# A windowed-attention and SwiGLU kernel: three warm-up matmuls rather than four, a fetch cut into head pairs, and other steps for weight casts, wo's powers and output stores

## The chip, the cores and the metric

The kernel runs on one core of a Trainium2 chip. The metric is the device time of one execution in microseconds (us); the profile that is read here shows one such execution, taken by the hardware profiler. The engines are TensorE (PE in the profile: matmuls; PEld: its weight loads), VectorE (DVE), ScalarE (ACT), GpSimd (POOL) and SyncE (SP), which here issues nearly all DMAs.

## The reference

x is 2048 tokens by 512 features, in fp32. Both branches read the same layer-normalised x.

```python
xn = _layernorm(x, axis=-1)
s = _A_ref(xn, A_wqkv, A_wo)        # 32 heads of 16
g = _silu(_B_ref(xn, B_w1, B_w3, B_w2))
return x + s * g
# _A_ref: q, k, v = xn @ wqkv;  scores = q k^T * 16 ** -0.5,
#   kept where 0 <= idx_q - idx_k < 256;  softmax over keys;  (p v) @ wo
# _B_ref: (silu(xn @ w1) * (xn @ w3)) @ w2,  1792 columns between
```

## The kernel before

**Precision.** A product of fp32 matrices is made of three fp16 matmuls: high by high, low by high and high by low halves (XH and XL are the halves of the normalised, transposed x). A weight tensor or a block of it is first scaled by a power of two. This power is measured on the chip: sums of squares per partition (`squares`, on ACT at line 249 and on DVE at line 251) go through a bf16 cast (line 261, DVE) and a small matmul with ones (`powers`, lines 280 and 285, PE), and a chain of small DVE instructions (lines 291 to 304) makes the power. Then the tensor is cut into halves. `split` does it in two instructions (line 333 on ACT, 334 on DVE); `split_pool` scales in place and casts the high half on ACT (lines 342 and 343) and makes the low half in four pieces on POOL (line 345).

**Tiling.** The tokens stand in 4 tiles of 512 (t). Attention has 4 groups of 8 heads (g), each with 2 passes of head pairs (p): 32 units (t, g, p). Q and K of a group are projected (`project`, matmuls at line 597, emptied at 614 by ACT and 618 by DVE), stored to DRAM in an expanded form (lines 619 to 625) and fetched back as tiles qa and KA (`fetch`, line 641). The first pass over the scores (`pass1`, matmuls at 665) finds row maxima on DVE (line 679); the second makes scores again (746), exponentials on ACT (756) and the product with V (774). The feed-forward branch works on 14 blocks of 128 columns (f): gate and up matmuls at 1036, emptied through ACT 1051, DVE 1055 and 1060 and ACT 1069; the down product is at 1261 for the first two token tiles and, with folded weights, at 1179 for the others. wo's product is at 1313.

**What sets the order.** PE's order is written by hand: a list of dense matmul pieces is spread between the score batches, and each piece is a step. `later(n, f)` runs f's code n steps on; `beside_scores(n, f)` puts f's small matmuls beside the first score batch after n steps. The other engines are ordered by a scheduler: it places an instruction by when it becomes ready, and by its place in the program where several are. `tc.issue_after(ins)` gives the instructions under it an order edge behind `ins`. The name `lasts["emptied"]` is set where a matmul bank is emptied, always to a DVE instruction (at line 618, for example).

**Buffers.** Two matmul banks (m) alternate, two double score tiles (s) alternate, and there is one more (po). 54 slots in SBUF hold weights and intermediate tiles: `take` gives the slot that has been free for longest, `give` frees one, some steps later where it says `after`. SP issues DMAs in order.

**The places that the change touches.** The prologue (from line 1531) runs warm-up matmuls with no useful product (`keep_busy`, line 1537), turns x by transposes (line 493, copied to XH by ACT at 496 and to XL by DVE at 501) and projects K and Q of group 0: k00 takes a score tile (line 594), q00 an m bank. `measure(f)` measures a pair of weight blocks f and f + 1 and calls `cut` four times, two for each block, at the steps that a tuple gives. `wout` prepares wo in unit 7. `total` (from line 1300) makes the output and stores it. The loads of w1 and w3 are at line 868, those of the later wqkv columns at 395, the stores of cut weights at 1042.

Of the kernel before, what the change touches and what calls it, by code (L numbers as in the profile page):

```python
# [10 lines left out]
F32 = mybir.dt.float32  # L11
# [10 lines left out]
P = 128  # L22
# [4 lines left out]
DH = 16  # L27
# [56 lines left out]
def tile_block(ctx: ExitStack, tc: tile.TileContext, x, wqkv, wo, w1, w3, w2, out):  # L84
# [35 lines left out]
    def give(*tiles, after=0):  # L120

        for made in tiles:
            given[0] += 1
            free.append((now[0] + after, given[0], held.pop(id(made))[0]))
# [38 lines left out]
    def bank(shape, dtype=F32):  # L163

        open_bank[0] = b = 1 - open_bank[0]
        return psm.tile(shape, dtype, name=f"m{b}", tag=f"m{b}", bufs=1)
# [414 lines left out]
    def project(t, g, k, terms=(range(3),), scores_bank=False):  # L581


        cell = {}

        parts = ([[(c, i) for c in (2 * half, 2 * half + 1) for i in range(3)] for half in range(2)] if len(terms) == 1
                 else [[(c, i) for i in group for c in range(NC)] for group in terms])

        def part(n):
            assert turned[t] == 4  # L590
            w = WQ[t, g, k]
            xh, xl = X[t]
            if n == 0:
                cell["pp"] = pss.tile([P, 2, TW], F32, name="s")[:, 0, :] if scores_bank else bank([P, TW])
            for c, i in parts[n]:
                a, b = ((0, xh), (1, xh), (0, xl))[i]
                nc.tensor.matmul(cell["pp"], w[:, (a * NC + c) * P:(a * NC + c + 1) * P], b[:, c, :], start=(c, i) == parts[0][0],  # L597
                                 stop=(c, i) == parts[-1][-1])
            if n < len(parts) - 1:
                return  # L600
            if t == 0:
                def store():
                    with behind_load():
                        nc.sync.dma_start(dWQ[g, k], w)
                    give(w, after=8)
                later(45, store)
            else:
                give(w)
            pp = cell["pp"]
            both = take(F16)  # L610
            B = both.rearrange("p (a t) -> p a t", a=2)
            s = QS / (XS * WS)
            with urgent():
                nc.scalar.activation(B[:, 0, :], pp, AF.Copy, scale=s)

            def rest():
                with urgent():
                    lasts["emptied"] = nc.vector.scalar_tensor_tensor(B[:, 1, :], pp, s, B[:, 0, :], op0=ALU.mult, op1=ALU.subtract)  # L618
                d = (dQ, dK)[k][g][:, :, t * TW:(t + 1) * TW]
                if k == 0:  # L620
                    nc.sync.dma_start(d[:, 0:2, :], B[:, 0:1, :].to_broadcast([P, 2, TW]))
                    nc.sync.dma_start(d[:, 2, :], B[:, 1, :])
                else:
                    nc.sync.dma_start(d[:, 0:2, :], B)
                    nc.sync.dma_start(d[:, 2, :], B[:, 0, :])
                give(both, after=4)
            later(1, rest)
        return opening([(len(l), lambda n=n: part(n)) for n, l in enumerate(parts)])
# [2 lines left out]
        WQ[t, g, k] = w = take(F16)  # L631
        nc.sync.dma_start(w, dWQ[g, k])

    def fetch(t, g):
        QA[t, g] = qa = qpool.tile([P, 4, TW], F16, name="qa")
        ka = keys(t, g)
        c0 = 0 if t else 2 * P
        for dst, d in ((ka[:, :, c0:], dK[g][:, :, t * TW - 2 * P + c0:(t + 1) * TW]),
                       (qa, dQ[g][:, :, t * TW:(t + 1) * TW])):
            for r in range(2):  # L640
                lasts["load"] = nc.sync.dma_start(dst[64 * r:64 * r + KR],
                                  d[64 * r:64 * r + 64].rearrange("(a d) i t -> (d i) a t", d=DH))

# [224 lines left out]

    measured = set()

    def measure(f, apart=0):

        raws = [RAW.pop(f + i) for i in range(2)]
        sb = squares([raws[0][0], raws[1][0], raws[0][1], raws[1][1]], on_act=4 if f > 2 else 2, apart=apart)

        def scale(s=None):
            pp = small.tile([P, 2, 2], F32, name="pp")
            pi = small.tile([P, 2, 2], F32, name="pi")  # L880
            return then(s, powers(sb, 4, pp.rearrange("p a b -> p (a b)"), pi.rearrange("p a b -> p (a b)"), s),
                        lambda: rest(pp, pi))

        def rest(pp, pi):
            ff = slice(f, f + 2)
            nc.vector.tensor_scalar(sg_scale[:, ff], pp[:, 0, :], 0.5 / (WS * XS), None, op0=ALU.mult)
            nc.vector.tensor_mul(p13[:, ff], pp[:, 0, :], pp[:, 1, :])
            measured.update((f, f + 1))

            def cut(i, k):  # L890
                if k == 0:
                    WF[0, f + i] = [[None, None], WF.pop((0, f + i), [None, None])[1]]
                WF[0, f + i][0][k] = a = take(F16)
                split_pool(a[:, 0:D], a[:, D:], raws[i][k], pi[:, k, i:i + 1])
                give(raws[i][k], after=5)
            for i in range(2):
                for k in range(2):
                    later(((1, 2, 4, 6) if f < 8 else (1, 5, 9, 13))[2 * i + k], lambda i=i, k=k: cut(i, k))
        if started:
            beside_scores(8, scale)  # L900
        else:
            later(10 if apart else 6, scale)

# [389 lines left out]
    def total(t, b):  # L1293

        r = slice(t * TW + b * P, t * TW + (b + 1) * P)
        cell = {}

        def part(half):
            WOH, WOL = SQ["wo"][:2]
            tb = slice(b * P, (b + 1) * P)  # L1300
            if half == 0:
                cell["ps"] = bank([P, D])
                assert (t, b) in summed
                cell["y"] = y = take(F32)
                acc = ACC[t, b]
                with behind_exp():
                    nc.scalar.activation(y, acc, AF.Tanh, scale=0.5)
                nc.vector.scalar_tensor_tensor(y, y, 1.0, acc, op0=ALU.add, op1=ALU.mult)
                give(acc)
            ps, y = cell["ps"], cell["y"]  # L1310
            for g in (2 * half, 2 * half + 1):
                for i, (a, w) in enumerate(((0, WOH), (0, WOL), (1, WOH))):
                    nc.tensor.matmul(ps, O[t, g][:, a, tb], w[g], start=g == 0 and i == 0,  # L1313
                                     stop=g == NG - 1 and i == 2)
            if half:
                with urgent():
                    lasts["emptied"] = nc.vector.scalar_tensor_tensor(y, ps, sc["y"], y, op0=ALU.mult, op1=ALU.mult)
                if t == NT - 1:
                    nc.vector.tensor_add(y, y, XR[t, b])
                else:  # L1320
                    halves(nc.gpsimd.tensor_add, y, y, XR[t, b])

                def store():
                    nc.sync.dma_start(out[r, :], y)
                    give(y, XR[t, b], after=30)
                if t == NT - 1:
                    store()
                else:
                    later(4, store)
                if b == 3:  # L1330
                    give(*(OT[t, g] for g in range(NG)))
        return opening([(6, lambda h=h: part(h)) for h in range(2)])
# [22 lines left out]
    def feed_forward():  # L1355
# [4 lines left out]
        for t in range(NT):  # L1360
            for f in range(FB):
                if t == 0:
# [3 lines left out]
                    elif f + LEAD == FB - 1:  # L1366
                        pieces += [(0, lambda f=f: load(0, f)) for f in range(FB - 2, FB)]
                    if f % 2 and f + 3 < FB:
                        pieces.append((0, lambda f=f + 3: later(5, lambda: measure(f, 1)) if f == 6 else measure(f, 1)))
                    pieces += [(0, lambda f=f: load_down(0, f)) for f in range(f + 2 if f else 0, min(f + 3, FB))]  # L1370
                    for m in range(f + 1 if f else 0, min(f + 2, FB)):
                        k = next(k for k, (_, f1) in enumerate(GROUPS) if m < f1)
# [158 lines left out]
        nc.gpsimd.memset(KA[2][:, a, :].bitcast(F32), TWO_ONES)  # L1531


    def keep_busy(n):
        ps = bank([P, 4, P])
        for _ in range(n):
            nc.tensor.matmul(ps, onesb, onesb.unsqueeze(1).to_broadcast([P, 4, P]), start=True, stop=True)

# [19 lines left out]
        flush()  # L1558
    with tc.issue_after(lasts["hi"].ins), tc.issue_after(lasts["x"].ins):
        qk[1][1]()  # L1560
    keep_busy(4)


    k00, q00 = (project(0, 0, k, ((0,), (1,), (2,)), k) for k in (1, 0))
    run([k00[0], q00[0], k00[1]])
    qk[1][2]()
    with tc.issue_after(lasts["scale"].ins):
# [2 lines left out]
    qk[1][3]()  # L1570
    with tc.issue_after(lasts["hi"].ins):
        run([k00[2], q00[2]])
    later(1, lambda: fetch(0, 0))
    k01 = project(0, 1, 1, ((0, 2), (1,)))
    run(k01[:1])
    wv[2]()
# [4 lines left out]
    sc["o"] = scaled(SQ["wv"][3], OS / WS, "so")  # L1581
    with tc.issue_after(lasts["hi"].ins):
        measure(0)
    run(project(0, 1, 0, scores_bank=True))
    later(1, lambda: fetch(0, 1))
    run(value(0, True))
    qk[2][1]()
# [35 lines left out]
    for n, u in enumerate(units):  # L1623
# [7 lines left out]
            wout[0]()  # L1631
        if n == 7:
            wout[1](2)
            beside_scores(12, lambda s: then(s, wout[2](s), lambda: later(2, lambda: wout[3](2)), lambda: later(3, out_scale)))
        want += a_unit - other[n]
        mine = more(want)

# [39 lines left out]
```

## Time and profile before

| | us |
|---|---|
| median of three runs | 811.76 |
| the three runs | 811.22, 811.76, 811.85 |
| the profiled execution | 811.24 |
| its span (first to last instruction) | 809.4 |
| PE busy in the span | 793.7 |
| DVE, ACT, POOL busy | 631.2, 392.1, 377.1 |
| granted TensorE clock | 1.00 |

1.84 us of the profiled execution lie outside the span. A timeline row shows start, duration, engine, line and operation, output and inputs, and in brackets the idle time of the engine just before it with what ended it. Matmul rows that follow one another are joined with a count (x4); their durations overlap, since a matmul starts before the one ahead of it has left the array. SPq stands for SP's queue of DMA issues.

### The profile page before, as it was taken

Reading aid. Unit: us, or ns where it says so; the run is one execution under the profiler, and the core shown is the slowest. Engines: PE = TensorE matmul, PEld = TensorE weight load, DVE = VectorE, ACT = ScalarE, POOL = GpSimd, SP = SyncE. Lnnn points to the kernel's source line nnn. Section 1 sums busy time; section 2 is a strip of 40 time slices with the busy share of each in tenths; the row PEclk is TensorE's granted clock in tenths of the full one; section 3 lists DMA queues with packets and bytes.
Section 4 is the critical chain, followed back from the end, with each engine's and each line's share of the span. In section 5 each row is a group of like instructions: output and inputs, shape, how many; then the busy total and the mean of one; then the engine's idle time right before and its main releaser. Section 6 shows DMA issues by size and latency. Waiting matters only on the chain.

```text
span 809.4 us, 23944 instructions
## 1 busy us (share of the span) xinstructions
PE 793.7 (98%) x9176; PEld 403.7 (50%) x9176; DVE 631.2 (78%) x2037; ACT 392.1 (48%) x591; POOL 377.1 (47%) x732
## 2 busy tenths in 40 slices
PE   8999989999999999999999999999999999999998
PEld 4444444444444444444444454456544754466465
DVE  8788788887888777887988888777778787875437
ACT  6879586553546544345344433344444234344411
POOL 2345376342329445354353455530346276550670
PEclk9999999999999999999999999999999999999999
DMA  9968554835576474757655634646372644335321
GB/s 282 265 214 267 160 183 134 278 114 191 160 199 208 134 232 139 218 142 263 160 162 181 194 104 119 185 137 179 105 201 74 160 139 137 113 90 172 111 65 62
DMA packets 109795, 134.19 MB, mean 166 GB/s; under 512 B 18864, under 2 KB 64880, under 8 KB 109680
## 3 DMA queue, kind: packets, MB, share of 16 engines
q1 hardware_dynamic: 109392, 132.13, 54.6%
q8 instruction: 72, 1.18, 0.6%
q10 hardware_dynamic: 288, 0.52, 0.2%
q14 instruction: 43, 0.35, 0.1%
HBM read 91.23 MB, written 36.57 MB: 158 GB/s over the span
## 4 chain that ended last, share of the span: by engine, by line
PE 79%; DVE 8%; ACT 6%; DMA 3%; issue 2%; SPq 1%; POOL 0%; ACTq 0%; DVEq 0%
PE m L1036 30%; PE po L774 8%; PE m L1261 8%; PE m L1179 8%; PE m L597 7%; PE s L746 5%; PE m L1313 4%; PE m L567 4%; PE s L665 3%; DMA slot<-in_B_w_dram 2%; DVE junk L679 2%; PE po L665 2%; ACT slot L342 1%; ACT pt L756 1%; ACT sqa L249 1%
## 5 line engine op out<-in xcount | busy, mean ns | idle before, releaser
L1036 PE MATMUL m<-XH,slot 128*128 128x512 f16 x896 | 267.4, 380 | 1.6 <-DVE slot L618 1.2
L756 ACT ACTIVATE pt<-s,es 128x1024 f32<-128x1024 f32 x152 | 167.5, 1112 | 193.7 <-DVE s L753 186.5
L1036 PEld LDWEIGHTS <-slot 128*128 128x128 f16 x1344 | 124.7, 98 | 156.0 <-issue 12.0
L1036 PE MATMUL m<-XL,slot 128*128 128x512 f16 x448 | 169.9, 379 | 0.0
L753 DVE TENSOR_TENSOR s<-s,MK 128x256 f32<-128x256 f32 (+2 forms) x280 | 118.7, 434 | 51.2 <-PE s L746 47.0
L679 DVE CUSTOM_DVE_ANT_0 junk<-s,MW 128x320 bf16<-128x320 f32 x276 | 133.9, 485 | 17.9 <-PE s L665 10.3
L339 POOL TENSOR_TENSOR slot<-slot,slot 128x256 f16<-128x256 f32 (+1 forms) x86 | 57.7, 692 | 141.9 <-ACT slot L1069 76.7
L345 POOL TENSOR_TENSOR slot<-slot,slot 128x128 f16<-128x128 f32 x168 | 69.1, 446 | 58.3 <-ACT slot L343 58.3
L679 DVE CUSTOM_DVE_ANT_0 junk<-po,MW 128x320 bf16<-128x320 f32 x172 | 83.4, 485 | 4.7 <-DVE mt L704 0.3
L1261 PE MATMUL m<-slot,slot 128*128 128x512 f16 x336 | 78.6, 380 | 0.3 <-DVE slot L1055 0.3
L774 PE MATMUL po<-pt,V 64*32 64x320 f32 (+4 forms) x2880 | 77.2, 342 | 0.8 <-DVE pp L304 0.8
L597 PE MATMUL m<-XH,slot 128*128 128x512 f16 x240 | 71.0, 380 | 1.6 <-DVE slot L1055 1.2
L1179 PE MATMUL m<-slot,slot 128*128 128x256 f16 x588 | 68.4, 273 | 0.0
L1094 POOL TENSOR_TENSOR slot<-slot,slot 128x256 f16<-128x256 f32 x98 | 64.6, 671 | 1.1
L1051 ACT ACTIVATE slot<-m,sgs 128x512 f32<-128x512 f32 x56 | 38.3, 683 | 54.4 <-PE m L1036 52.3
L774 PEld LDWEIGHTS po<-pt,V 64*32 64x32 f32 x2880 | 50.5, 106 | 22.9 <-PE s L515 0.9
L1179 PEld LDWEIGHTS <-slot 128*128 128x128 f16 x588 | 56.1, 98 | 11.5 <-issue 3.0
L1055 DVE SCALAR_TENSOR_TENSOR slot<-slot,m 128x512 f32<-128x512 f32 x56 | 38.3, 684 | 29.0 <-ACT slot L1051 29.0
L746 PE MATMUL s<-qa,KA 50*64 50x320 f16 (+3 forms) x1472 | 58.4, 260 | 0.1
L597 PEld LDWEIGHTS <-slot 128*128 128x128 f16 x384 | 35.6, 98 | 44.8 <-issue 3.4
L746 PEld LDWEIGHTS <-KA 50*64 50x64 f16 x1472 | 30.1, 106 | 51.9 <-issue 30.9
L1261 PEld LDWEIGHTS <-slot 128*128 128x128 f16 x336 | 30.7, 98 | 38.6 <-issue 4.2
(189 smaller groups left out, 1138.5 us busy)
## 6 DMA issues: line engine op xcount, KB each, us to landing
slot<-dW SPq DMA_DIRECT2D x98, 256.0 KB
slot<-in_B_w_dram SPq DMA_DIRECT2D x56, 256.0 KB
slot<-dFold SPq DMA_DIRECT2D x48, 256.0 KB
dW<-slot SPq DMA_DIRECT2D x42, 256.0 KB
slot<-in_A_x_dram SPq DMA_DIRECT2D x30, 256.0 KB
KA<-dK SPq DMA_DIRECT2D x24, 288.0 KB
qa<-dQ SPq DMA_DIRECT2D x32, 192.0 KB
slot<-dWQ SPq DMA_DIRECT2D x24, 256.0 KB
```

What stands on the lines that cost most here:

```text
L339: op(out[:, c], a[:, c], b[:, c])
L345: nc.gpsimd.tensor_sub(lo[:, c:c + P], raw[:, c:c + P], hi[:, c:c + P])
L597: nc.tensor.matmul(cell["pp"], w[:, (a * NC + c) * P:(a * NC + c + 1) * P], b[:, c, :], start=(c, i) == parts[0][0], stop=(c, i) == parts[ ...
L679: lasts["maximum"] = nc.vector.tensor_tensor_reduce(out=junk[:, :n], in0=s[:, r, :n], in1=mask, scale=1.0, scalar=NEG, op0=ALU.add, op1=AL ...
L746: nc.tensor.matmul(s[64 * h:64 * h + 64, r, o:o + 64 * n], ka[rows, 2 * p + a, 64 * (m + 4):64 * (m + 5)], qa[rows, 2 * p + a, 64 * (m + k ...
L753: nc.vector.tensor_add(v, v, MK[:, kind, of:of + n, :].unsqueeze(1).to_broadcast([P, 2 * len(which), n, 64]))
L756: lasts["exp"] = nc.scalar.activation(pt, s, AF.Exp, scale=es)
L774: nc.tensor.matmul(cell["po"][32 * i:32 * i + 32, h, 64 * (m + k):64 * (m + k + n)], V[64 * h:64 * h + 64, (4 * t + m // 2) % VB, hd * VW: ...
L1036: nc.tensor.matmul(cell[k], w[:, (a * NC + c) * P:(a * NC + c + 1) * P], b[:, c, :], start=c == 0 and i == 0, stop=c == NC - 1 and i == 2)
L1094: nc.gpsimd.tensor_sub(lo, view, hi)
L1179: nc.tensor.matmul(cell["ps"][:, c], made[:, f:f + P], wj[:, g:g + 256], start=j == j0 and c == 0 and n == 0, stop=j == j1 - 1 and n == 2, ...
L1261: nc.tensor.matmul(ps, hh[:, a * TW + b * P:a * TW + (b + 1) * P], w[:, c * D:(c + 1) * D], start=f == f0 and i == 0, stop=f == f1 - 1 and ...
```

## The change

The diff, cut to what the rest of the text speaks of; the projections `k00`, `q00` and the one at line 1584 pass their bank in another way, with the same bank as before.

```diff
-    def fetch(t, g):
+    def fetch(t, g, ps=None):
...
-        for dst, d in ((ka[:, :, c0:], dK[g][:, :, t * TW - 2 * P + c0:(t + 1) * TW]),
-                       (qa, dQ[g][:, :, t * TW:(t + 1) * TW])):
-            for r in range(2):
-                lasts["load"] = nc.sync.dma_start(dst[64 * r:64 * r + KR],
-                                  d[64 * r:64 * r + 64].rearrange("(a d) i t -> (d i) a t", d=DH))
+        for heads in (slice(0, 4),) if ps is None else [slice(2 * p, 2 * p + 2) for p in ps]:
+            for dst, d in ((ka[:, heads, c0:], dK[g][:, :, t * TW - 2 * P + c0:(t + 1) * TW]),
+                           (qa[:, heads, :], dQ[g][:, :, t * TW:(t + 1) * TW])):
+                for r in range(2):
+                    rows = slice(64 * r + DH * heads.start, 64 * r + DH * heads.stop)
+                    lasts["load"] = nc.sync.dma_start(dst[64 * r:64 * r + KR],
+                                      d[rows].rearrange("(a d) i t -> (d i) a t", d=DH))
...
-    def measure(f, apart=0):
+    def measure(f, apart=0, until=8):
...
+            def tied(i, k):
+                with tc.issue_after(lasts["emptied"].ins):
+                    cut(i, k)
             for i in range(2):
                 for k in range(2):
-                    later(((1, 2, 4, 6) if f < 8 else (1, 5, 9, 13))[2 * i + k], lambda i=i, k=k: cut(i, k))
+                    if f < 8:
+                        later((1, 2, 4, 6)[2 * i + k], lambda i=i, k=k: cut(i, k))
+                    else:
+                        later((1, 4, 13, 16)[2 * i + k], lambda i=i, k=k: tied(i, k))
         if started:
-            beside_scores(8, scale)
+            beside_scores(until, scale)
...
-                    later(4, store)
+                    later(10, store)
...
-                        pieces.append((0, lambda f=f + 3: later(5, lambda: measure(f, 1)) if f == 6 else measure(f, 1)))
+                        pieces.append((0, lambda f=f + 3: later(8, lambda: measure(f, 1, 6)) if f == 6 else measure(f, 1)))
...
-    keep_busy(4)
+    waiting = scores_bank()
+    keep_busy(3, waiting[:, 0, :].rearrange("p (k q) -> p k q", q=P))
...
-    later(1, lambda: fetch(0, 0))
+    later(1, lambda: fetch(0, 0, (0, 1)))
...
-            beside_scores(12, lambda s: then(s, wout[2](s), lambda: later(2, lambda: wout[3](2)), lambda: later(3, out_scale)))
+            beside_scores(14, lambda s: then(s, wout[2](s), lambda: later(2, lambda: wout[3](2)), lambda: later(3, out_scale)))
```

So the change does six things. Three warm-up matmuls, written to the score tile that k00 takes next, stand where four stood in an m bank. The first fetch, of group 0, loads KA and qa for two head pairs apart: 8 loads of half the size rather than 4. The measuring of the pair of blocks 6 and 7 begins 8 steps on rather than 5, and its small matmuls stand beside the first batch after 6 further steps rather than 8. The cuts of blocks 8 to 13 move from steps 1, 5, 9 and 13 to 1, 4, 13 and 16, under an order edge behind the last emptying of a bank. wo's powers move from 12 steps on to 14. Output stores of the first three token tiles are issued 10 steps on rather than 4.

Lines after the first hunks are up to 9 higher in the changed kernel (641 is 643, 679 is 681, 868 is 870, 1055 is 1063). The places at which its instructions stand otherwise follow.

SP's queue at the first fetch (dK and dQ are Q and K of a group in DRAM; 143, 147: group 0; 144, 148: group 1). Before:

```order
L625 DMA dK_147<-slot_408 128x512
L621 DMA dQ_143<-slot_417 128x2x512
L624 DMA dK_147<-slot_408 128x2x512
L622 DMA dQ_143<-slot_417 128x512
L395 DMA slot_551<-in_A_wqkv_dram 128x4x128
L625 DMA dK_148<-slot_462 128x512
L641 DMA KA_140<-dK_147 48x4x512 x2
L641 DMA qa<-dQ_143 48x4x512 x2
L624 DMA dK_148<-slot_462 128x2x512
```

And in the changed kernel, where the two load rows are followed by two more that read the same, for the second head pair:

```order
L625 DMA dK_147<-slot_406 128x512
L624 DMA dK_147<-slot_406 128x2x512
L621 DMA dQ_143<-slot_415 128x2x512
L622 DMA dQ_143<-slot_415 128x512
L625 DMA dK_148<-slot_464 128x512
L643 DMA KA_140<-dK_147 48x2x512 x2
L643 DMA qa<-dQ_143 48x2x512 x2
```

The load of a block of wqkv (395) no longer stands between the stores and the fetch; it is issued behind the stores of group 1, and so behind the fetch of both pairs.

DVE, around the bf16 cast of the squares of the second pair of blocks (sb, 128x2), in the first score batches. Before:

```order
L679 ISA junk,M<-s,M_106 128x256
L679 ISA M 128x1
L294 TENSOR_SCALAR al<-s 128x1
L261 CAST sb<-ssq 128x2
L679 ISA junk,M<-s,MW 128x320
L295 SCALAR_TENSOR_TENSOR al<-s,al 128x1
```

And in the changed kernel, some 18 rows further on:

```order
L334 SCALAR_TENSOR_TENSOR slot_726<-slot_205,sw_643,slot_726 128x512
L1063 SCALAR_TENSOR_TENSOR slot_737<-slot_737,m_716 128x512
L681 ISA junk,M<-s,MW 128x320
L681 ISA M 128x1
L261 CAST sb<-ssq 128x2
L681 ISA junk,M<-s,MW 128x320
```

The cast of sb is no longer ahead of four row maxima, two splits (334) and an emptying of a bank (1055, now 1063).

ACT, at the casts of a pair of blocks from 8 to 13 (a row in brackets names what the instruction waits for: an engine, or a landing of a DMA). Before:

```order
L1051 ACTIVATE slot_1827<-m_1805,sgs 128x512 [waits PE_49]
L342 ACTIVATE slot_1096<-slot_1096,pi 128x512 [waits DVE_49]
L342 ACTIVATE slot_1097<-slot_1097,pi 128x512
L343 CAST slot_1829<-slot_1096 128x512 [waits DMAHW7_49,Activation_49]
L343 CAST slot_1961<-slot_1097 128x512 [waits Activation_49,Pool_49]
L249 ACTIVATE sqa,ssq<-slot_1567 128x512 [waits DMAHW0_49]
L342 ACTIVATE slot_1100<-slot_1100,pi 128x512
L342 ACTIVATE slot_1101<-slot_1101,pi 128x512
L343 CAST slot_2064<-slot_1100 128x512 [waits Activation_49]
```

And in the changed kernel:

```order
L1059 ACTIVATE slot_1829<-m_1807,sgs 128x512 [waits PE_49]
L342 ACTIVATE slot_1098<-slot_1098,pi 128x512 [waits DVE_49]
L342 ACTIVATE slot_1099<-slot_1099,pi 128x512
L343 CAST slot_1831<-slot_1098 128x512 [waits DMAHW3_49,Activation_49]
L343 CAST slot_1916<-slot_1099 128x512 [waits DMAHW1_49,Activation_49]
L249 ACTIVATE sqa,ssq<-slot_1569 128x512 [waits DMAHW4_49]
L342 ACTIVATE slot_1102<-slot_1102,pi 128x512
L342 ACTIVATE slot_1103<-slot_1103,pi 128x512
L343 CAST slot_2171<-slot_1102 128x512 [waits DMAHW5_49,Activation_49]
```

The casts stand where they stood; they go to other slots, and two of them now wait for a landing of a DMA where they waited for POOL or for nothing outside ACT.

More of the change, by code (lines that the diff above doesn't have):

```diff
@@ L593, in part @@
             if n == 0:
-                cell["pp"] = pss.tile([P, 2, TW], F32, name="s")[:, 0, :] if scores_bank else bank([P, TW])
+                cell["pp"] = bank([P, TW]) if scores_bank is False else scores_bank()[:, 0, :]
             for c, i in parts[n]:
@@ L1531, in tile_block, with keep_busy @@
         nc.gpsimd.memset(KA[2][:, a, :].bitcast(F32), TWO_ONES)
-    def keep_busy(n):
-        ps = bank([P, 4, P])
+    def keep_busy(n, ps=None):
+        ps = bank([P, 4, P]) if ps is None else ps
         for _ in range(n):
@@ L1560, in tile_block @@
         qk[1][1]()
-    keep_busy(4)
-    k00, q00 = (project(0, 0, k, ((0,), (1,), (2,)), k) for k in (1, 0))
+    waiting = scores_bank()
+    keep_busy(3, waiting[:, 0, :].rearrange("p (k q) -> p k q", q=P))
+    k00, q00 = (project(0, 0, k, ((0,), (1,), (2,)), (lambda: waiting) if k else False) for k in (1, 0))
     run([k00[0], q00[0], k00[1]])
@@ L1583, in tile_block @@
         measure(0)
-    run(project(0, 1, 0, scores_bank=True))
+    run(project(0, 1, 0, scores_bank=scores_bank))
     later(1, lambda: fetch(0, 1))
```

## The prediction

> **What bounds the kernel now.** The page comes first: PE is busy for 98% of the span.
>
> ```profile
> span 809.4 us, 23944 instructions
> PE 793.7 (98%) x9176; PEld 403.7 (50%) x9176; DVE 631.2 (78%) x2037; ACT 392.1 (48%) x591; POOL 377.1 (47%) x732
> ```
>
> So 15.7 us of the span (809.4 - 793.7) are without a matmul, and nothing but these can be won, as the change removes one matmul of 0.22 us. The table of stretches shows where they lie.
>
> ```profile
> 40.00:60.00 20.00, 18.90 (x134) 8.05 (x133) 16.83 (x72) 15.60 (x35) 9.84 (x20) 1.00 0.69 217
> 60.00:80.00 20.00, 18.70 (x147) 8.24 (x146) 17.10 (x64) 18.92 (x37) 10.86 (x22) 1.00 0.83 267
> 300.00:600.00 300.00, 299.82 (x3714) 150.04 (x3720) 238.68 (x741) 128.75 (x167) 130.97 (x228) 1.00 0.57 166
> ```
>
> The second column is the stretch, the third PE. From 300 to 600 PE lacks 0.2 us; from 40 to 80 it lacks 2.4. In the early part ACT is nearly full as well (18.92 of 20), because the weights are cut there. PE's list of waits names what it waited for (us in all, times, longest):
>
> ```profile
> PE s L665 <- ACT pt L756: 2.4, 2, 1.6
> PE m L1036 <- DVE slot L618: 1.2, 2, 1.0
> PE s L665 <- DMA qa<-dQ: 0.4, 1, 0.4
> ```
>
> These are single events, each with an edit of the change near it or not. I go through them in time.
>
> **Warm-up and k00.**
>
> ```profile
> 11.67 0.60 PE L493 MATMUL s<-identf,slot 128*128 128x128 f32 x4
> 12.85 1.02 PE L1537 MATMUL m<-onesb 128*128 128x512 bf16 x4 [0.58 <-DVE XL L501]
> 13.71 1.03 PE L597 MATMUL s<-XH,slot 128*128 128x512 f16 x4
> 16.30 0.19 PE L280 MATMUL s<-sb,onesb 128*128 128x1 bf16 x2
> 12.41 0.62 ACT L496 CAST XH<-s 128x512 f16<-128x512 f32 x1
> 15.67 0.16 DVE L261 CAST sb<-ssq 128x2 bf16<-128x2 f32 x1
> ```
>
> The four warm-up matmuls wait 0.58 for DVE's read of their m bank, and k00 comes behind them at 13.71, though its last XH is there at 12.41 + 0.62 = 13.03. The score tile of the change has no such reader: three matmuls fit between 12.27 (11.67 + 0.60) and 13.0 at 0.215 each (13.71 - 12.85 over 4). k00 could start 0.63 earlier (13.71 - 13.08). But 2.59 behind it (16.30 - 13.71) stands L280, whose sb is cast on DVE until 15.67 + 0.16 = 15.83, behind work that does not depend on k00. With 0.05 for the start, 15.88 rather than 16.30 bounds the gain: **-0.42** (bounds -0.63 and 0). PE then runs without a gap to 29.5, so the gain is carried as far as the fetch.
>
> **The fetch in pairs.**
>
> ```profile
> 22.49 0.43 SPq L395 DMA_DIRECT2D slot<-in_A_wqkv_dram  x1
> 25.39 0.88 SPq L641 DMA_DIRECT2D qa<-dQ  x2
> 32.72 2.09 SPq L868 DMA_DIRECT2D slot<-in_B_w_dram  x4
> 29.50 0.24 PE L665 MATMUL s<-KA,qa 48*64 48x128 f16 x1
> 30.15 0.30 PE L665 MATMUL s<-KA,qa 48*64 48x128 f16 x7 [0.41 <-DMA qa<-dQ]
> 44.97 0.31 PE L665 MATMUL s<-KA,qa 48*64 48x128 f16 x8
> ```
>
> The last load of qa is issued at 26.27 and PE goes on at 30.15, so issue to use is at most 3.9 us; that bound serves again below. PE would need the tile at 29.50 - 0.42 = 29.08. The change makes the first pair's four loads half as large, and takes a load of 256 KB (L395 at 22.49) from ahead of them. No row shows such a half load, so its time is bounded: by nothing saved, which leaves the wait at 0.41 + 0.42 = 0.83 and gives the first gain back, and by half of 3.9 saved, which removes it. Needed is 0.83 of 3.9, a fifth, where the bytes fall by half: I take **-0.41**, wait gone. The second pair's loads come behind these on SP (four issues of 0.44, 1.76 in all) and so land by some 32, and the second pair is first read at 44.97. The four more issues also put SP's later loads back by 1.76 at most, those of weight blocks from 32.72 on first; I price this at 0, as a block is squared, scaled and cut before PE reads it, with 1.76 as its other end.
>
> The Trainium skill, "DMA: Bandwidth & Descriptors", section "Anatomy of one DMA", speaks against cutting a load up: it gives some 2.0 us for every DMA whatever its size, most of it spent on confirming the write, and only bytes / 436 GB/s on top (its fit is of POOL's path, not SP's). By an estimate from that page four halved loads of 192 KB save 0.4 MB / 436 GB/s = 0.9 us, just more than is needed, so the sum would stay; the trace does not separate the two parts.
>
> **The squares' cast and the stall at 55.** The diff moves measuring of blocks 6 and 7, and the order shows what that does to DVE: the cast of sb 128x2 leaves the place where DVE stands for it.
>
> ```profile
> 37.47 0.17 DVE L261 CAST sb<-ssq 128x2 bf16<-128x2 f32 x1 [1.60 <-ACT sqa L249]
> 44.27 0.69 DVE L1060 SCALAR_TENSOR_TENSOR slot<-m,slot 128x512 f32<-128x512 f32 x1
> 50.81 0.69 DVE L618 SCALAR_TENSOR_TENSOR slot<-m,slot 128x512 f16<-128x512 f32 x1 [1.42 <-ACT slot L614]
> 54.59 0.69 DVE L618 SCALAR_TENSOR_TENSOR slot<-m,slot 128x512 f16<-128x512 f32 x1
> 44.99 0.62 ACT L1069 CAST slot<-slot 128x512 f16<-128x512 f32 x1 [2.25 <-DVE slot L1060]
> 50.20 0.58 ACT L614 ACTIVATE slot<-m 128x512 f16<-128x512 f32 x1
> 53.65 0.58 ACT L614 ACTIVATE slot<-m 128x512 f16<-128x512 f32 x1
> 55.33 0.59 PE L1036 MATMUL m<-XH,slot 128*128 128x512 f16 x2 [1.03 <-DVE slot L618]
> ```
>
> DVE idles 1.60 for ACT's squares; seven us later L1060 is late by that, ACT idles 2.25 for L1060, its two L614 come late, and the bank that the second L618 empties (54.59 to 55.28) holds PE until 55.33. With the cast out of the way DVE starts the row maxima 1.6 earlier, L1060 and ACT's L1069 move up by some 2 us (1.6, and part of 0.83), and ACT's first L614 starts near 48.6 (50.20 - 1.6). Then DVE's first L618 starts near 49.2 rather than 50.81 (ACT's 48.6 plus 0.58), and the second stands 54.59 - 50.81 = 3.78 behind it, 52.97, since DVE is full between them. ACT's second L614 must be done by then: from the one L614 to the other ACT is full for 3.45 us (53.65 - 50.20), so it ends at 48.6 + 3.45 + 0.58 = 52.6, just in time. PE can go on at 52.97 + 0.69 + 0.05 = 53.7 rather than 55.33: 1.62, of which 0.83 was won before; the edit adds **-0.8**. Bounds: 0.2 lost, if ACT has a little more between the two than now and PE's gain shrinks on the way; and -1.03 - 0.2, the whole stall and its start-up.
>
> **The stalls after it.**
>
> ```profile
> 78.00:170.00 92.00, 86.34 (x1016) 42.06 (x1014) 75.64 (x287) 63.82 (x116) 49.24 (x119) 1.00 0.59 185
> 76.93 0.33 PE L665 MATMUL po<-KA,qa 48*64 48x320 f16 x4 [0.84 <-DVE M L679]
> 112.53 0.68 ACT L1051 ACTIVATE slot<-m,sgs 128x512 f32<-128x512 f32 x1
> 115.04 0.59 PE L597 MATMUL m<-XH,slot 128*128 128x512 f16 x2 [1.19 <-DVE slot L1055]
> 118.47 0.30 PE L665 MATMUL s<-KA,qa 48*64 48x256 f16 x4 [1.62 <-ACT pt L756]
> ```
>
> At 76.93 DVE's maxima are late behind ACT and L1055. ACT there gains the 2 us of its vanished wait, so this stall moves with PE; I put **+0.1** on it. From 78 to 170 PE lacks 5.7 us (92.00 - 86.34; the stalls at 115.04 and 118.47 are the largest), but DVE's and ACT's rows there read the same in both orders: I take it that what PE waits for there hangs on PE's earlier work and moves up with it; what it could gain or lose besides is in the rivals. **0.**
>
> **Casts of blocks 8 to 13.** The order edge is behind an instruction of DVE, the casts are on ACT and POOL, and ACT's rows at the casts are the same as before. So the edge holds nothing, and this part changes only which slots the casts write.
>
> ```profile
> 87.99 1.11 ACT L756 ACTIVATE pt<-s,es 128x1024 f32<-128x1024 f32 x1 [8.03 <-DVE s L753]
> 103.48 1.45 SPq L1042 DMA_DIRECT2D dW<-slot  x2
> 105.87 1.12 ACT L343 CAST slot<-slot 128x512 f16<-128x512 f32 x2
> 108.75 1.12 ACT L343 CAST slot<-slot 128x512 f16<-128x512 f32 x2
> 110.91 1.11 ACT L756 ACTIVATE pt<-s,es 128x1024 f32<-128x1024 f32 x1 [0.35 <-DVE s L753]
> ```
>
> A slot that was freed lately is one whose store may still be on its way. If the store issued at 104.93 takes the 3.9 us of the fetch, it lands at 108.8; the second cast, at 106.4 (105.87 + 0.5), would be 2.4 late, the third, at 108.75, not at all. Behind it on ACT stand L1069 and L756 with 0.35 to spare, so the price of a pair is 0 to 2.05 (2.4 - 0.35), and there are three pairs. I take **0**, since slots are taken oldest first and so most stores landed long before; 2.05 to 6 goes into a rival. The same page's 2.0 us and bytes / 436 GB/s would put this store's landing at 104.93 + 2.6 = 107.5 (an estimate), 1.1 late; no run shows it so far.
>
> **wo's powers and output stores: 0.** wo is first needed at 305.4, its casts now end at 246; one score batch later costs nothing of 59 us.
>
> ```profile
> L1313 PE MATMUL m<-slot,slot x24: 378/379/391, 305.4 to 325.6; 128*128 128x512 f16 x24
> L343 ACT CAST slot<-slot x4: 602/610/620, 242.4 to 245.9; 128x512 f16<-128x512 f32 x4
> ```
>
> (Columns: min, median and max ns, first and last start.) The stores of tiles 0 to 2 are not read again, and the last tile keeps its place; without that cover a slot would come free 6 steps late, some 8 us of one of 54.
>
> **Sum.** -0.42 - 0.41 - 0.8 + 0.1 = -1.53: the span goes from 809.4 to 807.9. The profiled execution has 811.24, 0.52 under the median of the runs; against the median the forecast is 811.76 - 1.53 = **810.2 us**. This kernel's measurement tells about 0.2% (1.62 us) from no change, so the forecast stands just inside that bound.
>
> **Rivals.**
>
> *The gain is caught up.* ACT has 18.92 busy of 20 between 60 and 80. If ACT, not the wait for sb, sets the pace from 48 to 77, PE arrives earlier and waits longer; for it speaks the full ACT, against it the 2.25 that ACT idles at 44.99. What is left is the prologue or less: 811.0 to 811.8.
>
> *More is won.* The stalls of 55 and 77 vanish whole (0.2 + 0.84 more), and those from 100 to 131 shrink, because ACT comes to them with its 2 us ahead of PE: ACT's part is the 2.4 of PE's two waits for L756. For it: these are waits on ACT. Against it: ACT idles 8.03 us before 87.99, so a lead does not last. Up to -1.53 - 1.04 - 2.4, so 806.8 to 809.3.
>
> *Slower: casts behind a store.* The mechanism above, on ACT, from the point where a slot's store lands after about 106.7 (cast's time plus 0.35). One to three pairs at 2.05, less 1.53 won: 812.3 to 816.4, middle 814.3. For it: two rows of the order wait for a landing where none was waited for. Against it: slots are taken oldest first.
>
> *The edge works after all.* If something holds the casts behind the bank, they no longer delay L1051 and L756 at 112 to 118: part of the 1.19 + 1.62 lost there is won. The order speaks against it; it counts with "more is won".
>
> **How the numbers follow.** Forecast 0.45, with its own range 809.2 to 811.1 (the term of 0.8 between its ends, the others between half and whole); caught up 0.15; more won 0.20; slower 0.20. Of the forecast's case a bit less than half lies below 810.14 (811.76 - 1.62), and a little of it could be lost in the spread of 0.6 between runs. Faster by over 0.2%: 0.22 + 0.20 = 0.42; within: 0.23 + 0.15 = 0.38; slower: 0.20. The range takes the forecast, the caught-up case, most of the larger gain and the lower half of the slower case: 807.4 to 813.4.
>
> **What would show it.** Right: k00 starts at 13.1 and L280 at 15.9; the wait for qa at 29 to 30 is gone; DVE has no idle of over 1 us between 35 and 38; the stall on L618 near 54 is under 0.5; stalls of 1.2 and 1.6 stand 1.5 us earlier than 115 and 118. Wrong: ACT rows L343 that idle for a DMA near 105, 120 or 135, a wait for qa that stays, or stalls after 60 that have grown by what was won before.

## The result and the profile after

The changed kernel takes 815.33 us (median of five runs, 814.71 to 816.05), against 811.56 for the kernel before beside it: slower, by a ratio of 1.0048 (95% interval 1.0034 to 1.0062). The profiled execution is the median run, with a span of 813.5. The prediction had said 810.2, so it was wrong in sign: 5.1 us are to be accounted for.

Some kernels had runs of 817 to 822 us (2 of the 10 of wo12; 4 of the 10 of w_tie, whose other six took 808.9 to 810.5) with a mean granted clock of 0.994 to 0.996; medians over all runs are quoted, and what makes these runs was not found.

PE's list of waits, of the profile after (lines behind the first hunks are up to 9 higher: 665 is 667, 756 is 758, 1036 is 1044, 1055 is 1063):

```profile
PE s L667 <- ACT pt L758: 3.3, 4, 1.6
PE m L1044 <- DVE slot L1063: 2.2, 2, 1.9
PE s L748 <- ACT pt L758: 1.5, 1, 1.5
PE m L1044 <- DVE slot L618: 0.8, 2, 0.6
```

The waits for the warm-up's bank and for qa are gone from the list; a wait of 1.5 for exponentials and one of 1.9 for an emptied bank are new. The timeline of PE shows where they stand. In the first part it is what was forecast:

```profile
13.15 1.02 PE L597 MATMUL s<-XH,slot 128*128 128x512 f16 x4 [0.17 <-ACT XH L496]
15.96 0.20 PE L280 MATMUL s<-sb,onesb 128*128 128x1 bf16 x2
29.17 0.60 PE L667 MATMUL s<-KA,qa 48*64 48x128 f16 x8
53.72 0.59 PE L1044 MATMUL m<-XH,slot 128*128 128x512 f16 x2 [0.65 <-DVE slot L618]
113.26 0.59 PE L597 MATMUL m<-XH,slot 128*128 128x512 f16 x2 [0.83 <-DVE slot L1063]
116.69 0.30 PE L667 MATMUL s<-KA,qa 48*64 48x256 f16 x4 [1.63 <-ACT pt L758]
```

Against the same instructions in the kernel before: L280 0.34 earlier (16.30), the bank of L618 1.61 earlier (55.33), the two stalls behind 112 each 1.78 earlier (115.04 and 118.47). At 237 us PE is 1.94 ahead (a score matmul that starts at 237.93 before starts at 235.99). Then, still in PE's timeline:

```profile
258.46 0.42 PE L748 MATMUL s<-qa,KA 50*64 50x320 f16 x12 [1.47 <-ACT pt L758]
259.35 0.42 PE L748 MATMUL s<-qa,KA 50*64 50x320 f16 x12 [0.47 <-DVE XL L525]
264.64 0.59 PE L1044 MATMUL m<-XH,slot 128*128 128x512 f16 x2 [1.86 <-DVE slot L1063]
267.26 0.33 PE L667 MATMUL s<-KA,qa 48*32 48x320 f16 x8 [0.74 <-ACT pt L758]
532.67 2.75 PE L1321 MATMUL m<-slot,slot 128*128 128x512 f16 x12 [0.57 <-DVE slot L1063]
```

In the kernel before, PE's list of waits is empty between 170 and 700. Its rows at two of these places are

```profile
259.76 0.33 PE L665 MATMUL po<-KA,qa 48*64 48x320 f16 x4
264.30 2.53 PE L774 MATMUL po<-pt,V 64*32 64x256 f32 x96
```

The same matmuls start at 259.75 and 267.40 in the changed kernel. So the first two stalls use up the lead, and the next two make a lag of 3.1; the one at 532 brings the lag to 3.85, and there it stays. ACT and DVE show what is late. ACT first:

```profile
247.70 1.33 ACT L342 ACTIVATE slot<-slot,swwo 128x512 f32<-128x512 f32 x2 [0.82 <-DVE swwo L302]
252.28 1.11 ACT L758 ACTIVATE pt<-s,es 128x1024 f32<-128x1024 f32 x1
253.29 0.61 ACT L343 CAST slot<-slot 128x512 f16<-128x512 f32 x1
253.80 0.72 ACT L999 ACTIVATE slot<-slot,fw 128x512 f32<-128x512 f32 x1
254.42 0.61 ACT L1077 CAST slot<-slot 128x512 f16<-128x512 f32 x1
254.93 0.72 ACT L999 ACTIVATE slot<-slot,fw 128x512 f32<-128x512 f32 x1
255.55 0.58 ACT L614 ACTIVATE slot<-m 128x512 f16<-128x512 f32 x1
257.29 1.11 ACT L758 ACTIVATE pt<-s,es 128x1024 f32<-128x1024 f32 x1 [1.16 <-DVE s L755]
```

The same work in the kernel before (its first scaling of wo, its last cast of wo, and L614):

```profile
241.23 0.72 ACT L342 ACTIVATE slot<-slot,swwo 128x512 f32<-128x512 f32 x1
245.95 0.62 ACT L343 CAST slot<-slot 128x512 f16<-128x512 f32 x1
255.49 0.60 ACT L614 ACTIVATE slot<-m 128x512 f16<-128x512 f32 x1 [0.16 <-PE m L597]
```

wo's scaling and casts (swwo is wo's power) ran from 241.23 to 246.57 and now begin at 247.70. They keep ACT full until 253.9, the folding work (L999) comes behind them, and the read of a bank at L614, for which ACT had waited on PE, starts at 255.55, no earlier than before, though PE is almost 2 us ahead. DVE and POOL at that place:

```profile
256.17 0.69 DVE L618 SCALAR_TENSOR_TENSOR slot<-m,slot 128x512 f16<-128x512 f32 x1 [1.90 <-ACT slot L614]
259.61 4.05 DVE L824 TENSOR_SCALAR dr<-dr,so 128x32 f32<-128x32 f32 x1
263.92 0.67 DVE L1063 SCALAR_TENSOR_TENSOR slot<-slot,m 128x512 f32<-128x512 f32 x1
```

```profile
258.28 0.40 POOL L1014 CAST slot<-slot 128x256 f16<-128x256 f32 x1
258.63 0.72 POOL L1002 TENSOR_TENSOR slot<-slot,slot 128x256 f32<-128x256 f32 x1
...
261.37 1.92 POOL L1015 TENSOR_TENSOR slot<-slot,slot 128x256 f16<-128x256 f32 x3
263.24 0.40 POOL L1014 CAST slot<-slot 128x256 f16<-128x256 f32 x1
263.71 0.67 POOL L1015 TENSOR_TENSOR slot<-slot,slot 128x256 f16<-128x256 f32 x1
```

DVE idles 1.90 for L614: the whole lead is lost there. And a scaling of 128x32 elements takes 4.05 us. It begins while POOL works without a break, and it ends at 263.66, in POOL's first break (263.64 to 263.71). L1063, which empties PE's bank, stands behind it on DVE. In the kernel before, the same scaling began at the same time, also beside a busy POOL, and took 0.52:

```profile
259.62 0.52 DVE L822 TENSOR_SCALAR dr<-dr,so 128x32 f32<-128x32 f32 x1
259.37 0.74 POOL L1006 CAST slot<-slot 128x256 f16<-128x256 f32 x2
260.06 1.93 POOL L1007 TENSOR_TENSOR slot<-slot,slot 128x256 f16<-128x256 f32 x3
```

So two costs were to be told apart, both near 260. By these rows both come from the move of wo's powers, which the prediction had put at 0; the experiments test that.

### The profile page after: what moved, and what is told of

The parts are those of the page before. It is cut to its first block, busy times and chain, and to the rows that moved or that the text cites. A ratio compares the mean times of both kernels' runs of the same rounds, so it can differ in the third digit from the quotient of the medians.

```text
span 813.5 us, 23978 instructions
## 1 busy us (share of the span) xinstructions
PE 794.2 (98%) x9175; PEld 404.5 (50%) x9175; DVE 635.9 (78%) x2037; ACT 391.7 (48%) x591; POOL 378.0 (46%) x732
## 5 line engine op out<-in xcount | busy, mean ns | idle before, releaser
L755 DVE TENSOR_TENSOR s<-s,MK 128x256 f32<-128x256 f32 (+2 forms) x280 | 118.8, 435 | 50.2 <-PE s L748 47.0
L1063 DVE SCALAR_TENSOR_TENSOR slot<-slot,m 128x512 f32<-128x512 f32 x56 | 38.3, 685 | 28.8 <-ACT slot L1059 27.4
```

The lines of the kernel that those rows point to most:

```text
L755: nc.vector.tensor_add(v, v, MK[:, kind, of:of + n, :].unsqueeze(1).to_broadcast([P, 2 * len(which), n, 64]))
```

## The experiments

**wo's move alone.** wo12 takes this edit back in the changed kernel; only_wo14 makes it alone in the kernel before.

```diff
wo12, against the changed kernel:
-            beside_scores(14, lambda s: then(s, wout[2](s), ...
+            beside_scores(12, lambda s: then(s, wout[2](s), ...
only_wo14, against the kernel before:
-            beside_scores(12, lambda s: then(s, wout[2](s), ...
+            beside_scores(14, lambda s: then(s, wout[2](s), ...
```

> The changed kernel with wo's powers put back to 12 steps on. Theory (wo's preparation costs it all, by 258 to 268 us and by what follows): the four stalls of the profile after at 258.46, 259.35, 264.64 and 267.26 (4.54 us together) go, PE stays the 1.9 us ahead that it has at 237 us to the end: 809.5 to 810.0. Rival (the casts of blocks 8 to 13 or the later stores cost it, and the stalls near 260 are their echo): 814 to 815.5.

> The kernel before with nothing but wo's powers put to 14 steps on. Theory (wo alone): about 4.5 to 5.8 slower than before, 816 to 817.4, with the stalls near 260 as in the profile after. Rival (it takes wo's move together with the other parts): within 1 us of before.

wo12: 810.41 us (kernel before 811.32; ratio 1.0009, 0.9983 to 1.0036). only_wo14: 816.45 (1.0063, 1.0048 to 1.0078). So wo's move costs 5.1 us without any of the other edits (816.45 - 811.32) and 4.9 with them (815.33 - 810.41); the rest of the change is a gain of about 0.9. In only_wo14 both costs are there again without the other edits: PE is 1.85 behind the kernel before at the first place above and 4.96 at the second (261.61 for 259.76, 269.26 for 264.30). DVE's long instruction ends where POOL breaks off:

```profile
261.47 4.06 DVE L822 TENSOR_SCALAR dr<-dr,so 128x32 f32<-128x32 f32 x1
```

```profile
265.09 0.40 POOL L1006 CAST slot<-slot 128x256 f16<-128x256 f32 x1
265.57 1.30 POOL L1007 TENSOR_TENSOR slot<-slot,slot 128x256 f16<-128x256 f32 x2
```

It ends at 265.53, between 265.49 and 265.57. wo12 is 0.4 to 0.9 above what was expected, and its PE timeline shows one reason: PE, now earlier, comes to wo's powers at 12 steps before their sb is cast.

```profile
236.40 0.28 PE L285 MATMUL s<-sb,onesb 64*64 64x1 bf16 x12 [0.57 <-DVE sb L261]
```

**DVE's scaling of 4 us.** no_so leaves out this instruction (its output lacks the factor so); so_act makes it on ACT.

```diff
 no_so and so_act, against the changed kernel:
-                nc.vector.tensor_scalar(dr, dr, sc["o"], None, op0=ALU.mult)
 so_act only:
+                nc.scalar.activation(dr, dr, AF.Copy, scale=sc["o"])
```

> The changed kernel without the small DVE instruction that scales the reciprocals of the softmax sums by so (16 of them, 0.24 us each as a rule); its output lacks this factor. Theory A (the one that takes 4.05 us near 260 us, beside a full POOL, is a cost of its own): the stalls at 264.64 and 267.26 go or shrink, 812 to 813. Theory B (wo's casts on ACT ahead of the emptying of a bank at line 614 make the whole loss, and DVE would wait anyway): less than 0.7 us won, 814.5 to 815.3.

> The changed kernel with the scaling of the reciprocals by so on ACT in place of DVE (16 small instructions). Theory (the 4.05 us near 260 us are DVE's instruction held up by POOL's unbroken row of instructions): no instruction of this scaling takes over 0.5 us on ACT, the stall at 264.64 goes, 811 to 812 as in no_so. Rival (what is waited for there is the data, on whatever engine it is): the same 3 to 4 us appear as a wait on ACT, 815.

no_so: 811.54 (810.71 to 813.1), 3.8 below the changed kernel: theory A, and 0.5 under its range. The stalls at 264, 267 and 532 are gone; the one at 258 and that of 0.47 behind it stay, and PE is level with the kernel before at 259 us (first row). POOL's row is the same to 0.01, and the DVE instructions that stood behind the scaling now run beside it at their usual length (L755 at 259.60 in 0.43, then the emptying of the bank at 259.93 in 0.68):

```profile
258.44 0.42 PE L748 MATMUL s<-qa,KA 50*64 50x320 f16 x12 [1.40 <-ACT pt L758]
```

So 3.8 go with the instruction: the 3.1 of the stalls behind it and the 0.7 at 532, whose link to it is open. ACT's lateness takes the lead of 1.9. so_act: 814.46, well above its 811 to 812, though the sign that it was to show is there: no stall at 264, and no long scaling. All instructions of the scaling (min, median, max in ns; first so_act, then the changed kernel):

```profile
L824 ACT ACTIVATE dr<-dr,so x16: 305/321/322, 123.3 to 784.5; 128x32 f32<-128x32 f32 x16
```

```profile
L824 DVE TENSOR_SCALAR dr<-dr,so x16: 234/241/4053, 123.0 to 784.3; 128x32 f32<-128x32 f32 x16
```

Beside the same row of POOL work the longest is 0.32 on ACT and 4.05 on DVE, so it isn't the data that is waited for: it is DVE that is held up. What so_act gives back lies elsewhere: a spell of half clock from 260.6 to 263.6 in its profile (1.7 us, see the last section), and a new stall of 1.7 near 529, where PE waits for a bank that ACT reads (L570), behind the scaling on ACT's queue. Less these two the profiled 815.61 would be 812.2 (an estimate).

**The other edits, taken back one at a time from wo12.**

```diff
w_warm4:
-    waiting = scores_bank()
-    keep_busy(3, waiting[:, 0, :].rearrange("p (k q) -> p k q", q=P))
+    keep_busy(4)
w_fetch1:
-    later(1, lambda: fetch(0, 0, (0, 1)))
+    later(1, lambda: fetch(0, 0))
w_meas5:
-... later(8, lambda: measure(f, 1, 6)) if f == 6 ...
+... later(5, lambda: measure(f, 1)) if f == 6 ...
w_cuts:
-                        later((1, 4, 13, 16)[2 * i + k], lambda i=i, k=k: tied(i, k))
+                        later((1, 5, 9, 13)[2 * i + k], lambda i=i, k=k: cut(i, k))
store4, against the changed kernel:
-                    later(10, store)
+                    later(4, store)
```

> wo12 with the old warm-up: four matmuls in an m bank before k00. My term of 0.42: L280 back from 15.8 to about 16.3, 0.4 to 0.5 lost there and carried to 115 us; the time 810.4 to 810.9. Rival (DVE or a DMA sets the pace behind it): 0.4 lost at 16 but nothing left by 60 us, and the time of wo12 (810.4).

w_warm4: 811.81, 1.4 above wo12. The rows answer in two steps (DVE, then PE):

```profile
36.97 0.42 DVE L261 CAST sb<-ssq 128x2 bf16<-128x2 f32 x1 [0.54 <-ACT sqa L249]
```

```profile
55.09 0.59 PE L1044 MATMUL m<-XH,slot 128*128 128x512 f16 x2 [1.27 <-ACT slot L333]
```

L280 is 0.67 later than in wo12, of which 0.21 stand already at 5.5 us, in the first warm-up matmuls that both have: 0.46 for the forecast 0.42. But then the cast of sb is back between the row maxima, DVE waits for it, and PE is 1.49 later at 55. The move of that cast, which the prediction had put down to the measuring of blocks 6 and 7, belongs to the prologue. A likely reason is that the scheduler orders by readiness, and that an earlier PE makes the maxima ready first; no run tests that.

> wo12 with the first fetch whole. My term of 0.41: PE's wait for qa comes back near 29 us, of 0.4 to 0.8, so PE is 0.35 to 0.4 later at 30 us; the time 810.4 to 810.9. Rival (another order of SP ahead of it does it, not the halves): no wait comes back, same time as wo12.

w_fetch1: 811.10, 0.7 above wo12. Its PE rows:

```profile
29.86 0.24 PE L667 MATMUL s<-KA,qa 48*64 48x128 f16 x1 [0.71 <-DMA qa<-dQ]
30.80 0.30 PE L667 MATMUL s<-KA,qa 48*64 48x128 f16 x7 [0.70 <-DMA qa<-dQ]
```

Two waits, 1.41 together, come back where the prediction had 0.41, or 0.83 with the prologue's gain given back. SP's queue ahead of the fetch is that of wo12, so it is the halves that remove the wait, and the rival is out. The last whole load of qa is issued at 26.11, 0.16 earlier than in the kernel before, and PE goes on at 30.80, 0.65 later than there: what holds the loads up is open. Of the 1.41, 0.5 come back at 236, where PE, now later, no longer waits for wo's powers.

> wo12 with the measuring of blocks 6 and 7 at 5 and 8 steps on as before. My term of 0.8: DVE idles about 1.6 again at 36 to 38 us, the stall on L618 near 54 is over 1 us, and PE is 0.6 to 0.9 later at 56 us; the time 810.8 to 811.3. Rival (the gain at 55 comes from the earlier prologue alone): PE at 56 us within 0.2 of wo12.

w_meas5: 810.41, the same as wo12, and the bank of L618 at the same time (wo12 has 53.60):

```profile
53.64 0.59 PE L1044 MATMUL m<-XH,slot 128*128 128x512 f16 x2 [0.62 <-DVE slot L618]
```

DVE's idle time does not come back. The rival holds: this edit is worth nothing here.

> wo12 with the casts of blocks 8 to 13 at steps 1, 5, 9 and 13 and without the order edge. My reading (the edge holds nothing, only slots differ): PE within 0.2 of wo12 at every place where the clock is full, the time within 0.4 of 810.4. Rival (casts into slots whose store is late hold ACT near 115): the stalls near 113 and 117 shrink by over 0.5.

w_cuts: 810.25, within 0.2 of wo12. Every engine and SP's queue have the same instructions in the same order in both; the stalls at 113 and 117 are of 0.83 and 1.63 in both. The edge on DVE's instruction holds nothing, and no cast waits for a store.

> The changed kernel with output stores 4 steps on as before. Theory (stores cost nothing): within 0.4 us of the changed kernel, 815.0 to 815.7, the stall of 0.57 at 532.67 stays or goes with it. Rival (the later stores stand in SP's queue before what the reciprocals wait for near 528 us): 0.6 to 0.9 faster, 814.5.

store4: 815.37, against 815.33. Nothing. The stall of 0.57 near 532 isn't in it, but waits of 1.0 for loads of dWQ near 340 to 364 are; what the stall is owed to stays open.

**Two that go on from wo12.** w_tie names ACT's own last read of a bank in the edge; w_sq1 makes wo's squares one step apart, so that its sb is cast earlier; w_tie_sq1 is both.

```diff
w_sq1, w_tie_sq1:
-            wout[1](2)
+            wout[1](1)
w_tie, w_tie_sq1:
-                nc.scalar.activation(B[:, 0, :], pp, AF.Copy, scale=s)
+                lasts["read"] = nc.scalar.activation(B[:, 0, :], pp, AF.Copy, scale=s)
...
-                    nc.scalar.activation(sg, cell[0], AF.Tanh, scale=sg_scale[:, f:f + 1])
+                    lasts["read"] = nc.scalar.activation(sg, cell[0], AF.Tanh, scale=sg_scale[:, f:f + 1])
...
-                with tc.issue_after(lasts["emptied"].ins):
+                with tc.issue_after(lasts["read"].ins):
```

> wo12 with wo's squares one step apart in place of two. Theory (the one loss of wo12 against the lead of 1.9 us is PE's wait of 0.6 for wo's sb at 236 us): the wait goes, PE stays 1.7 to 1.9 ahead of before to the end, 809.6 to 809.9 where the clock is full. Rival: the squares on DVE then delay other work by as much, 810.4 as wo12.

> wo12 with the order edge of the casts of blocks 8 to 13 behind ACT's own last read of a bank (lines 614 and 1059) in place of DVE's. Theory (an edge holds only instructions of the engine that it names): now ACT's casts do move behind those reads; the stalls near 113 and 117 (0.8 and 1.6 in wo12) shrink by 0.5 to 2, 808.5 to 810. Rival (the stalls hang on DVE and on the squares, not on the casts): they stay, 810.4, or the casts come late for POOL and other stalls grow, over 811.

> w_sq1 with the order edge of w_tie. If the two gains add: PE 0.5 further ahead than w_sq1 behind 113 us, 809.2. If the edge's gain is given back further on (a stall of 0.6 near 527 in w_tie) or its late casts cost more in some runs (four of ten runs of w_tie took 817 and more): 809.7 or a spread up to 818.

w_sq1: 809.67 (809.47 to 809.99; ratio 0.9968, 0.9941 to 0.9995). The cast of sb stands at 229.91 rather than 236.19, and PE's wait at L285 is gone. w_tie: 810.04, just above its 808.5 to 810. The edge now does what its name says: the casts leave their place, and the stall at 113 shrinks, here in w_tie_sq1:

```profile
112.67 0.59 PE L597 MATMUL m<-XH,slot 128*128 128x512 f16 x2 [0.19 <-DVE slot L1063]
116.11 0.30 PE L667 MATMUL s<-KA,qa 48*64 48x256 f16 x4 [1.63 <-ACT pt L758]
```

The second, of 1.63, does not; and w_tie has a stall of 0.62 at 527.9 that w_tie_sq1 has not. w_tie_sq1: 809.31 (808.91 to 809.97), ratio 0.9973 (0.9962 to 0.9983) to the kernel before: faster than both kernels of this case, by 2.0 and 6.0 us.

## The prediction, step by step

**Warm-up, -0.42: right.** 0.34 in the trace (16.30 to 15.96) and 0.46 in w_warm4.

**Fetch in pairs, -0.41: right in its mechanism, too small.** The wait is gone, and without the edit it is 1.41, not 0.41 or 0.83: with the prologue earlier, PE comes 0.4 earlier to whole loads that then come 0.65 later. In time it is 0.7, since part of it is given back at 236.

**The squares' cast and the stall at 55, -0.8: right in place and size, booked under the wrong edit.** PE went on at 53.72 (53.7 forecast), DVE's idle time is gone; the stall left there is 0.65, where under 0.5 had been named as the sign. But w_meas5 shows that the measuring of blocks 6 and 7 has no part in it, and w_warm4 that the prologue has: the warm-up edit is worth 1.4 in all, the measuring nothing. That the sum came out is luck, as both edits were in the change.

**Stalls after it, +0.1 and 0: right.** The two large ones stand 1.78 earlier, and PE is 1.94 ahead at 237 for a forecast of 1.53.

**Casts of blocks 8 to 13, 0: right**, and so the rival by which casts wait behind a store is out. It was the slower case of the prediction; that its times (812.3 to 816.4) hold the result is luck, as its reason was not at work.

**wo's powers, 0: this step failed, and alone decides.** "wo is first needed at 305.4, its casts now end at 246; one score batch later costs nothing of 59 us." The slack is real, but it is that of PE, which reads wo at 305.4. The step looked at who waits for the moved work, and not at who stands behind it in the queues: eight instructions on ACT, sixteen on POOL. The move was also taken for one score batch; but the chain of small DVE instructions runs on later steps, and wo's power came at 247.6 rather than 241.1, 6.5 later, with PE 1.9 earlier. On ACT the casts then stand ahead of L614 (DVE idles 1.90, the lead is gone), and on POOL the sixteen pieces push the folding work into an unbroken row beside DVE's scaling (3.8). Both show as another order on ACT and POOL; the prediction read the order for its other edits and not for this one. ACT's part could have been priced that way. The 3.8 could not: in the trace of before no scaling took over 0.85. **The stores, 0:** right by store4.

The sum of what the runs show: 1.9 won until 237, 1.9 lost to ACT, 3.1 to DVE's scaling, 0.7 at 532, which is 3.8 slower; measured are 3.8 (815.33 - 811.56). The times have a spread of some 0.5, and the spells of half clock lie within the times of the experiments; so the split is good to about half a microsecond. No run moves ACT's casts alone; their part is what no_so leaves.

## What to carry to other kernels

A moved block of work has two slacks: that of whoever reads it, and that of whatever it is put in front of on each in-order queue; a price of nothing needs both, engine by engine. An engine that is under half busy, as POOL is here, can still hold up another while it works without a break, and by how much a row of the old trace need not tell. An order edge is worth a look at the order: if it names an instruction of another engine, it may hold nothing.

## What the runs showed of the hardware

**DVE held up behind POOL.** The scaling (fp32, 128x32, SBUF to SBUF) takes 0.24 us as a rule. In each of the twelve kernels that have it on DVE, five of the sixteen take longer, and each of these ends 0.04 behind the end of a POOL instruction. In the kernel before, the one of 0.52 ends at 260.14 and POOL's second cast at 260.11 (259.37 + 0.74). All but three get through at the first or second such end after their start, in 0.45 to 0.87. The three are the scaling near 260, of 4.04 to 4.06, in the kernels with wo's powers at 14 steps and the scaling on DVE (the changed kernel, only_wo14, store4): there it lets seven ends pass and gets through at the eighth, which is POOL's first break. In the other nine kernels this same scaling takes 0.45 to 0.78. The reciprocal just before it (0.35 at 257.51) and the row maxima between them ran beside the same work at their usual length. The Trainium skill, "SBUF — State Buffer", section "Who interferes with whom", has a pair of ports that DVE's two-port modes and GpSimd share; the one that issues first holds it for its whole instruction, with the other blocked, and tensor_scalar is among the instructions that can use such a mode. The rows agree that DVE waits for the end of a POOL instruction, and by them the wait can outlast several. Why the scaling gets through at the second end in the kernel before and at the eighth in the changed one, no run here shows; a break of POOL is not needed for it, as the row of before has none there.

**Spells of half clock.** In the profile of wo12 the pitch of PE's matmuls is 0.43 us rather than 0.215 from 118.3 to 121.5, behind the stalls of 0.83 and 1.63; the table of stretches (clock third from the end):

```profile
116.00:118.00 2.00, 1.41 (x43) 1.09 (x43) 0.78 (x3) 2.00 (x5) 1.60 (x5) 0.97 0.09 23
118.00:120.00 2.00, 2.00 (x7) 0.61 (x5) 1.97 (x9) 2.00 (x4) 1.65 (x4) 0.50 0.75 239
120.00:122.00 2.00, 2.00 (x8) 0.81 (x7) 1.37 (x5) 2.00 (x6) 1.18 (x4) 0.67 0.10 32
```

The profile of w_sq1 has the same stalls there and a clock of 1.00. In wo12 the 1.7 us were given back, since the stalls behind them at 122.7 and 128.6 vanished (at 128.5 PE was level with the profile after again); in no_so and so_act, where such a spell lies at 260.6 to 264, they were not. The Trainium skill, "TensorE: Matmul & The Clock Gate", section "What's actually happening", halves the clock after an idle window of some 3.4 us that runs freely, which fits a spell of 3.2 us that comes in one execution and not in the next; here, though, a stretch that was not wholly idle was enough: in the 3.4 us ahead of the spell PE was busy for 1.77 in wo12 (114.9 to 118.3) and for 1.69 in no_so (257.2 to 260.6).
